# Single thresholds, leftovers loaded two tiles ahead, and a fixed order for VectorE's softmax from tile 98

## The chip, the cores and the metric

The kernel runs on one core of one Trainium2 chip. The metric is the device time of one execution in microseconds (us), the median of several runs. Beside it stands one profiled execution, in which a hardware profiler recorded the instructions of every engine: TensorE (PE, with its weight loads as PEld), VectorE (DVE), ScalarE (ACT), GpSimd (POOL) and SyncE (SP), which issues most of the loads and stores.

## What is computed

Attention with a relative threshold, and behind it a mixture of experts in which every token goes to one expert. Batch 8, 8 heads, 576 positions, head size 64; the 4608 tokens have 512 columns, and there are 8 experts with 1024 hidden columns.

```python
scores = scale * np.matmul(q, k.transpose(0, 1, 3, 2))
thresh = np.max(scores, axis=-1, keepdims=True) - tau
scores = np.where(scores >= thresh, scores, -1000000000.0)
attn = np.exp(scores - np.max(scores, axis=-1, keepdims=True))
attn = attn / (np.sum(attn, axis=-1, keepdims=True) + 1e-09)
x = (attn @ v)                       # to (4608, 512)
logits = x @ w_gate + modality_bias[modality_id]
e_idx = np.argmax(logits, axis=1)    # gate_w: softmax of logits at e_idx
for e in range(E):
    h = np.maximum(x[e_idx == e] @ w1[e], 0.0)
    out[e_idx == e] = gate_w[e_idx == e, None] * (h @ w2[e])
```

## The kernel before, in words

Attention runs in 288 **tiles**, numbered from 0, of 128 rows of scores by 576 keys. Nine tiles make a pair of heads: eight of the 512 main rows of the two heads, and one with the 64 leftover rows of both. Pair p begins at tile 9p, four pairs make a batch. A loop runs through the tiles. In tile n TensorE makes the scores (`qk_half`, line 428) in one of two PSUM buffers, `s2[n % 2]`, so that the scores of tile n+2 wait until tile n has been masked. Then follow, on VectorE the negated row **maximum** (line 461), on ScalarE the exponential (line 471), on VectorE the **threshold** (line 468, one column) and the **mask** (line 485), which multiplies the exponentials by "score >= threshold", sums the rows and is the last reader of the scores. Two tiles later TensorE transposes the masked tile (`tr`, line 513), and after each half of a pair it multiplies by v (`pv_half`, line 547).

From tile 2 to 97 the loop goes by pairs of tiles (`two` is true): the masks of an even tile and the odd one behind it are issued together. There the maxima, thresholds and masks carry an order token ("softmax"), so that VectorE keeps them in the order of the program. Up to tile 63 (`LEAD`) both thresholds of such a pair of tiles stand behind the second maximum; from 64 to 97 one small sum (line 464) makes both. From tile 98 there is no token: a planner places the instructions of VectorE, ScalarE and SP by its own estimate, while TensorE and GpSimd run in the order of the program.

**Preparing a pair** (`prep_steps`): TensorE transposes the leftovers of k and q (`kq_r`, line 351), then the main keys and queries (`k_m`, `q_m`, line 365); GpSimd splits them into high and low parts (lines 339, 340); SP copies these into place (lines 374, 380). `load_qk`, called five tiles before the preceding pair begins, issues the loads of the leftovers (line 115) and then the main ones (line 124), all on SP.

**The experts** run between the attention's instructions. After each batch the routing (`route_a`, `route_b`, `route_c`) writes the tokens' places into a table. Seven times, for a slot that begins at tile n0 (64, 100, 136, 175, 214, 253, 292), `pick` **chooses** the expert with the most waiting tokens, in eight small instructions on VectorE over eight values (lines 732 to 743), asked for at tile n0 - 14 without a token. SP reads the choice into registers; GpSimd gathers the tokens' rows (line 855) by a list that SP loads (line 839); TensorE transposes them (line 869) and multiplies by both weights (lines 915 and 942). The first layer's result leaves PSUM as a high part by ScalarE (line 926) and a low part by VectorE (line 927). The first slot has 256 tokens and two gathers, asked for 6.4 and 6.3 tiles before it begins.

**Banks**: `tbank` hands out four PSUM banks in turn, the one used longest ago first. `let_go` returns a bank that was held over several steps and puts it at the end of the line. `x_out`'s `rest` takes a bank for one small transpose (line 617), which VectorE scales (line 630).

Of the kernel before, what the change touches and what calls it, by code (L numbers as in the profile page):

```python
# [29 lines left out]
def tile_attn_moe(  # L30
# [14 lines left out]
    C = {'prep': [0, 1, 2], 'tr0': 6, 'pv0': 7, 'tr1': 12, 'sums': 13, 'pv1': 13, 'x': 14, 'gate': [15, 16, 17, 18], 'route': 18, 'routeb': 21, 'E0': 28, 'lag': 3, 'first': ((1, 0), (1, 1), (1, 2), (1, 3), (2, 0)), 'lld': {(1, 5): 15, (1, 6): 15.6, (1, 7): 16.2, (2, 5): 16.8, (2, 6): 17.4, (2, 7): 18}, 'late': ((1, 5), (1, 6), (1, 7), (2, 5), (2, 6), (2, 7)), 'pick': -14, 'vld': 6, 'qkld': -5, 'pre': 2.5, 'wl': 3.5, 'rows': -11, 'gat': [-9.5, -8.5, -7, -5], 'xt': [-6, -5, -4, -2], 'lc': 21, 't3': 84, 'neg': 1.0, 'draw': [2, 2, 2, 2, 1, 2, 2, 1, 2], 'last': 36, 'part': 84, 'join': 11, 'drawj': [2, 2, 2, 2, 2, 2, 0, 2, 2], 'gatej': [15, 15, 17, 18], 'te': 8, 'f0': 19, 'sc': 1, 'warm': 24,  # L45
         'wS': [-6, -4.7, -3.4, 3, 12.5, 14, 15.5, 21.5, 4.2, 5.4, 6.6, 7.5, 22.7, 23.8, 24.9, 25.8],
         'wL': [-5.5, -4, -2.5, 2.7, 12, 13.3, 14.6, 21, 3.8, 4.9, 6, 7.1, 15.8, 22.2, 23.4, 24.6], 'ask': 4, 'gat0': [-6.4, -6.3], 'xt0': [-2, -1], 'rows0': -9.6, 'gat1': [-9.6, -9.5, -5], 'fill': (8, 8.5), 'fpool': (3,), 'route0': (18, 18, 20), 'pair1': 5, 'rest1': 19, 'gap': (1.0, 0.75), 'exp': -12.5, 'two': 98, 'end': (12, 13, (15, 16), (13.5, 13.6, 14.1, 14.2), 14.5, 15, 16.5), 'xf': 9, 'early': [], 'parts': ((((7, 0, 2), (9, 2, 5)), ((11, 0, 2), (13, 2, 5))), (((6, 0, 2), (8, 2, 4), (10, 4, 5)), ((12, 0, 2), (14, 2, 5)))), 'xp': ((15, 16), (16, 17)), 'prepp': ((0, 1, 2), (0, 0, 2)), 'trp': ((7, 11), (6, 12))}
# [59 lines left out]
    def load_qk(p):  # L107
        b, j = p // NPAIR, p % NPAIR
        tiles = []
# [4 lines left out]
        for z, src in enumerate((k, q)):  # L114
            nc.sync.dma_start(out=r[z * R:(z + 1) * R], in_=src[b, 2 * j:2 * j + 2, SA:S, :].rearrange("s r d -> r s d"))
        for z, (nm, src) in enumerate((("k", k), ("q", q))):
# [190 lines left out]
    def tbank(hold=False):  # L307
        i = next(x for x in line if x not in held)
        line.remove(i)
        line.append(i)  # L310
        if hold:
            held.add(i)
        return banks[i]

    def let_go(t):
        for i in range(4):
            if banks[i] is t:
                held.discard(i)
                line.remove(i)
                line.append(i)  # L320
# [126 lines left out]

    def softmax_a(n, two):
# [12 lines left out]
        in_line(nc.vector.tensor_reduce(out=nm[:, 0:1], in_=sv, axis=AX.XY, op=ALU.max, negate=True), two)  # L461
# [16 lines left out]
    def softmax_b(n, two):  # L478
        p, i = n // NI, n % NI
        e, th = soft.pop(n)[1], soft.pop((n, "th"))  # L480
# [6 lines left out]
            in1=e, op0=ALU.is_ge, op1=ALU.mult, accum_out=rs[:, ia:ia + 1]), two)  # L487
# [104 lines left out]
    def x_out(p):  # L592
# [136 lines left out]
    def pick(w):  # L729

        a = tiny.tile([1, NE], F32, name="pk_a", bufs=1)
        nc.vector.scalar_tensor_tensor(out=a, in0=done, scalar=float(-U * TS), in1=base[0][0:1, :],
                                       op0=ALU.mult, op1=ALU.add)
# [559 lines left out]
```

## Time and profile before

| | before |
|---|---|
| runs, us | 1015.66, 1016.04, 1013.46 |
| median, us | 1015.66 |
| profiled execution, us | 1014.53 |
| its span from first to last instruction, us | 1012.8 |
| busy share of PE, DVE, ACT, POOL | 97%, 67%, 63%, 52% |
| mean granted TensorE clock | 0.998 |

The span is what the profile's rows cover; the execution's own time holds 1.7 us more. TensorE is nearly always busy, so the reader should look for the moments in which it is not, and for what ended each of them.

### The profile page before, as it was taken

What the parts mean: (1) busy time and instruction counts of PE and PEld (TensorE: products, weight loads), DVE (VectorE), ACT (ScalarE), POOL (GpSimd) and SP (SyncE); (2) the same over time, 40 slices, a digit from 0 to 9 for tenths busy, and PEclk for the clock granted to TensorE, in tenths of its full rate; (3) what the DMA queues carried; (4) which work ended last, traced back from release to release, by engine and by line L of the source; (5) the groups of instructions that cost most, each with busy time, mean ns of one, the idle gap of its engine ahead of it and who ended that gap; (6) DMA issues with size and microseconds to landing.
All of it is one profiled execution on the core that took longest, in us unless ns stands there. A gap on an engine that the chain in (4) does not pass through costs nothing.

```text
span 1012.8 us, 20320 instructions
## 1 busy us (share of the span) xinstructions
PE 986.9 (97%) x6556; PEld 795.0 (78%) x6556; DVE 681.9 (67%) x1696; ACT 634.7 (63%) x1448; POOL 527.6 (52%) x733
## 2 busy tenths in 40 slices
PE   7999999999998999999999999999999999999997
PEld 6777678778887887888778887788878868888885
DVE  6888977787677776777677777777676765333422
ACT  6777787776666666666667666666666635334430
POOL 4354466386537554645546554646567374534311
PEclk9999999999999999999999999999999999999999
DMA  6667587678646765575645656567665336634301
GB/s 157 154 151 171 142 186 187 171 181 203 169 127 158 195 158 148 125 201 158 181 110 143 166 157 152 140 155 198 166 154 141 95 92 181 222 103 143 105 20 44
DMA packets 207139, 152.22 MB, mean 150 GB/s; under 512 B 100110, under 2 KB 168078, under 8 KB 207024
## 3 DMA queue, kind: packets, MB, share of 16 engines
q1 hardware_dynamic: 199776, 131.74, 51.2%
q0 software_dynamic: 7248, 19.09, 6.1%
q8 instruction: 54, 0.88, 0.4%
q14 instruction: 61, 0.50, 0.2%
HBM read 80.05 MB, written 19.87 MB: 99 GB/s over the span
## 4 chain that ended last, share of the span: by engine, by line
PE 79%; issue 8%; DVE 7%; DMA 2%; POOL 2%; ACT 1%; SPq 1%; POOLq 0%; DVEq 0%; ACTq 0%
PE s L428 15%; PE bk L547 15%; PE bk L513 11%; PE bk L942 11%; PE bk L915 10%; PE pm L942 5%; PE pm L915 4%; PE bk L365 2%; DVE nm L461 2%; DVE pr L485 2%; PE bk L538 2%; PE bk L869 1%; PE bk L599 1%; PE bk L646 1%; DMA k_m<-in_k_dram 1%
## 5 line engine op out<-in xcount | busy, mean ns | idle before, releaser
L461 DVE TENSOR_REDUCE nm<-s 128x1 f32<-128x576 f32 x254 | 190.9, 752 | 101.7 <-PE s L428 94.0
L485 DVE SCALAR_TENSOR_TENSOR pr<-s,nm,e 128x576 f32<-128x576 f32 x254 | 204.8, 815 | 61.6 <-ACT e L471 56.1
L471 ACT ACTIVATE e<-s,nm 128x576 f32<-128x576 f32 x254 | 188.4, 743 | 59.8 <-DVE nm L461 49.8
L428 PE MATMUL s<-km,q 128*128 128x288 f32 x1024 | 196.5, 313 | 10.6 <-DVE pr L485 9.7
L523 ACT COPY ptm<-bk 128x512 f32<-128x512 f32 x256 | 149.3, 583 | 53.4 <-PE bk L513 49.5
L513 PE MATMUL bk<-ident,pr 128*128 128x128 f32 x1152 | 173.8, 273 | 0.0
L428 PEld LDWEIGHTS s<-km,q 128*128 128x128 f32 x1024 | 146.4, 189 | 27.7 <-DVE pr L485 22.2
L513 PEld LDWEIGHTS bk<-ident,pr 128*128 128x128 f32 x1152 | 140.6, 140 | 27.2 <-issue 6.2
L547 PE MATMUL bk<-ptm,v_m 128*64 128x320 f32 (+1 forms) x1024 | 140.7, 412 | 0.0
L901 POOL TENSOR_TENSOR w2l<-raw,w2h 128x512 fp32r<-128x512 f32 x77 | 98.3, 1286 | 32.6 <-ACT w2h L897 28.5
L547 PEld LDWEIGHTS bk<-ptm,v_m 128*64 128x64 f32 x1024 | 68.2, 136 | 50.5 <-issue 8.2
L957 POOL DMA_INDIRECT out_dram<-y,tb x37 | 37.6, 1017 | 122.2 <-DVE y L955 92.8
L502 ACT COPY rp<-pr 128x64 f32<-128x64 f32 x271 | 59.9, 248 | 41.8 <-DVE pr L485 36.6
L339 POOL CAST nk<-str 128x64 fp32r<-128x64 f32 x31 | 7.4, 238 | 144.7 <-ACT str L353 140.5
L915 PE MATMUL bk<-xh,w1h 128*128 128x512 f32 (+3 forms) x204 | 82.2, 403 | 0.1
L915 PE MATMUL bk<-xh,w1l 128*128 128x512 f32 (+3 forms) x204 | 74.1, 363 | 0.0
L915 PE MATMUL bk<-xl,w1h 128*128 128x512 f32 (+3 forms) x204 | 74.0, 363 | 0.0
L942 PE MATMUL bk<-w2h,hh 128*128 128x512 f32 x168 | 73.3, 437 | 0.0
L901 POOL TENSOR_TENSOR w1l<-raw,w1h 128x512 fp32r<-128x512 f32 x53 | 68.1, 1285 | 4.2
L942 PE MATMUL bk<-w2h,hl 128*128 128x512 f32 x168 | 66.3, 395 | 0.0
L942 PE MATMUL bk<-w2l,hh 128*128 128x512 f32 x168 | 66.1, 393 | 0.0
L901 DVE TENSOR_TENSOR w1l<-raw,w1h 128x512 fp32r<-128x512 f32 x27 | 19.3, 720 | 59.4 <-ACT w1h L897 53.3
(217 smaller groups left out, 1999.5 us busy)
## 6 DMA issues: line engine op xcount, KB each, us to landing
raw<-in_moe_w_dram SPq DMA_DIRECT2D x160, 256.0 KB
q<-nq SPq DMA_DIRECT2D x124, 256.0 KB
km<-nk SPq DMA_DIRECT2D x124, 144.0 KB
v_m<-in_v_dram SPq DMA_DIRECT2D x32, 256.0 KB
xs<-xr SPq DMA_DIRECT2D x32, 256.0 KB
k_m<-in_k_dram SPq DMA_DIRECT2D x62, 128.0 KB
q_m<-in_q_dram SPq DMA_DIRECT2D x62, 128.0 KB
vr<-in_v_dram SPq DMA_DIRECT2D x64, 16.0 KB
```

Source lines behind the costliest of these rows:

```text
L428: nc.tensor.matmul(out=sps[:, hf, 0:SH], lhsT=a, rhs=x, start=(z == 0), stop=(z == len(passes) - 1))
L461: in_line(nc.vector.tensor_reduce(out=nm[:, 0:1], in_=sv, axis=AX.XY, op=ALU.max, negate=True), two)
L471: in_line(nc.scalar.activation(out=e, in_=sv, func=AF.Exp, bias=nm[:, 0:1]), two and n < LEAD)
L485: in_line(nc.vector.scalar_tensor_tensor(out=pr.rearrange("p (a x) -> p a x", a=2), in0=s2[n % 2][:, :, 0:SH], scalar=th, in1=e, op0=ALU.i ...
L502: (nc.gpsimd.tensor_copy if 2 <= n < 46 else nc.scalar.copy)(out=state[("rp", p)][:, 2 * c + s + x, :], in_=pr[:, SA:S])
L513: nc.tensor.transpose(out=ps[:, kc * P:(kc + 1) * P], in_=pr[:, kc * P:(kc + 1) * P], identity=ident)
L523: in_line(nc.scalar.copy(out=ptm[:, s, :, (c % 2) * P:(c % 2 + 1) * P], in_=pv), n + 2 < LEAD)
L547: nc.tensor.matmul(out=o, lhsT=lhsT, rhs=rhs, start=start, stop=stop, skip_group_check=True)
L901: then(eng.tensor_tensor(out=lo, in0=raw, in1=hi.bitcast(F32), op=ALU.subtract), eng is nc.vector and (lined or late))
L915: nc.tensor.matmul(out=ps[:, 0:WT], lhsT=a[:, cs], rhs=x[:, c, :], start=(c == 0 and z == 0), stop=(c == KC - 1 and z == 2))
L942: nc.tensor.matmul(out=ps, lhsT=h[:, ts], rhs=w, start=(z == 0 and y == 0), stop=(z == F2 - 1 and y == 2))
L957: i = _inst(nc.gpsimd.indirect_dma_start(out=out, out_offset=bass.IndirectOffsetOnAxis(ap=tb[:, t, 0:1].bitcast(U32), axis=0), in_=y, in_o ...
```

## The change

Five things change.

- **Thresholds.** In tiles 2 to 63 each tile has its threshold by itself: an even tile's directly behind its maximum, an odd tile's directly ahead of its mask and so behind the even tile's mask.
- **Order.** All maxima, thresholds and masks carry the token, from tile 98 too, where they stand as maximum, threshold, mask, tile by tile.
- **The choice.** `pick` is cut into three parts, asked for at n0 - 15, n0 - 14 and n0 - 13 (before: all at n0 - 14) and placed with the late work of a tile, behind its mask; its instructions carry the token.
- **Loads.** From pair 2 on the two loads of the leftovers are asked for seven tiles before the preceding pair begins, not five (`load_rest`). The two gathers of the first slot are asked for at 8.4 and 8.3 tiles before it, not 6.4 and 6.3.
- **Banks.** From tile 98, if the bank at the end of the line was just let go, `rest` puts its own bank ahead of that one.

```diff
-'pick': -14, ... 'gat0': [-6.4, -6.3]
+'pick': (-15, -14, -13), ... 'gat0': [-8.4, -8.3]
...
+    def load_rest(p):
...
+        loads[("kq_r", p)] = r
...
+        if p == 1:
+            load_rest(p)
+        r = loads.pop(("kq_r", p))
...
-    def tbank(hold=False):
+    freed = []
+
+    def tbank(hold=False, quick=False):
         i = next(x for x in line if x not in held)
         line.remove(i)
         line.append(i)
+        if quick and line[-2] in freed:
+            line[-2:] = [i, line[-2]]
...
                 held.discard(i)
+                freed[:] = [i]
...
+    def threshold(n, nm2, two):
+        y = cols(n % 2)
+        in_line(nc.vector.tensor_scalar(out=nm2[:, 1, y], in0=nm2[:, 0, y], scalar1=-1.0, scalar2=ntau,
+                                        op0=ALU.mult, op1=ALU.add), True)
...
-        in_line(nc.vector.tensor_reduce(out=nm[:, 0:1], in_=sv, axis=AX.XY, op=ALU.max, negate=True), two)
+        in_line(nc.vector.tensor_reduce(out=nm[:, 0:1], in_=sv, axis=AX.XY, op=ALU.max, negate=True), True)
...
-        for y in () if summed or two and n % 2 == 0 else (0, 1) if two else (n % 2,):
-            in_line(nc.vector.tensor_scalar(out=nm2[:, 1, cols(y)], in0=nm2[:, 0, cols(y)], scalar1=-1.0, scalar2=ntau,
-                                            op0=ALU.mult, op1=ALU.add), two)
+        if not (summed or two and n % 2):
+            threshold(n, nm2, two)
...
+        if two and n < LEAD and n % 2:
+            threshold(n, soft[n][0], two)
...
-            in1=e, op0=ALU.is_ge, op1=ALU.mult, accum_out=rs[:, ia:ia + 1]), two)
+            in1=e, op0=ALU.is_ge, op1=ALU.mult, accum_out=rs[:, ia:ia + 1]), True)
...
-                ps = tbank()
+                ps = tbank(quick=step[0] >= C['two'])
...
-    def pick(w):
+    def pick(w, out):
...
+        def which():
...
+        def place():
...
+        def take():
...
+        return which, place, take
...
+            if p:
+                at(n0 + (-7), lambda p=p: load_rest(p + 1))
             at(n0 + C['qkld'] if p else 0, lambda p=p: load_qk(p + 1))
...
-        def choose(cells=cells, w=w):
-            cells["c"] = pick(w)
-        at(n0 + C['pick'], choose)
+        def choose(z, cells=cells, w=w):
+            if z == 0:
+                cells["f"] = pick(w, cells)
+            cells["f"][z]()
+        for z, t in enumerate(C['pick']):
+            put(n0 + t, lambda z=z, choose=choose: choose(z))
```

`which` holds the old lines 732, 734, 736 and 742, `place` 737, 739 and 741, `take` 743.

## Rows read from the trace of the kernel before

**Rows 1.** Stages: us, busy us of PE, PEld, DVE, ACT, POOL; clock; DMA.

```profile
0.00:145.00 145.00, 132.52 (x1031) 101.94 (x1031) 122.57 (x330) 109.34 (x238) 69.42 (x177) 1.00 0.68 160
145.00:238.00 93.00, 91.72 (x693) 74.37 (x694) 69.27 (x170) 65.88 (x165) 59.28 (x74) 1.00 0.74 186
238.00:810.00 572.00, 568.14 (x3931) 462.45 (x3929) 413.94 (x1046) 386.45 (x909) 316.98 (x408) 1.00 0.60 155
810.00:1012.80 202.80, 194.52 (x906) 156.23 (x904) 76.15 (x153) 73.00 (x137) 81.89 (x76) 0.99 0.37 114
```

**Rows 2.** TensorE's waits, 0 to 145 us: us in total, times, longest.

```profile
PE s L428 <- DVE pr L485: 6.8, 11, 1.5
...
PE bk L351 <- DMA kq_r<-in_q_dram: 0.8, 1, 0.8
...
PE bk L365 <- DMA k_m<-in_k_dram: 0.6, 1, 0.6
```

**Rows 3.** TensorE's waits, 145 to 238 us.

```profile
PE s L428 <- DVE pr L485: 0.7, 1, 0.7
PE bk L365 <- DMA k_m<-in_k_dram: 0.5, 1, 0.5
```

**Rows 4.** TensorE's waits, 238 to 810 us.

```profile
PE s L428 <- DVE pr L485: 2.4, 2, 2.1
PE bk L351 <- DVE hl L927: 1.1, 2, 0.6
```

**Rows 5.** VectorE's timeline, tiles 17 to 19: start us, length us, instruction, count.

```profile
45.57 0.81 DVE L485 SCALAR_TENSOR_TENSOR pr<-s,nm,e 128x576 f32<-128x576 f32 x1
...
46.69 1.58 DVE L461 TENSOR_REDUCE nm<-s 128x1 f32<-128x576 f32 x2
48.30 0.34 DVE L468 TENSOR_SCALAR nm<-nm,ntau 128x1 f32<-128x1 f32 x2
48.65 0.82 DVE L485 SCALAR_TENSOR_TENSOR pr<-s,nm,e 128x576 f32<-128x576 f32 x1
```

**Rows 6.** TensorE's timeline, scores of tiles 19 and 20; in brackets, idle before.

```profile
46.70 0.77 PE L428 MATMUL s<-km,q 128*128 128x288 f32 x4
...
49.53 0.80 PE L428 MATMUL s<-km,q 128*128 128x288 f32 x4 [0.34 <-DVE pr L485]
```

**Rows 7.** Line 468, all thresholds: ns minimum/median/maximum, first and last start.

```profile
L468 DVE TENSOR_SCALAR nm<-nm,ntau x254: 175/213/217, 9.6 to 808.3; 128x1 f32<-128x1 f32 x127
```

**Rows 8.** SP's timeline near 137 us.

```profile
136.58 2.26 SPq L115 DMA_DIRECT2D kq_r<-in_k_dram  x1
```

**Rows 9.** GpSimd's timeline, 131 to 135 us.

```profile
131.84 0.61 POOL L339 CAST nq<-st 128x512 fp32r<-128x512 f32 x1 [1.52 <-ACT st L368]
...
133.95 1.09 POOL L855 DMA_INDIRECT xg<-xs,tb  x1
```

**Rows 10.** VectorE's timeline, 304 to 308 us, tiles 121 to 123.

```profile
304.34 1.14 DVE L737 TENSOR_SCALAR pk_a<-iota,pk_r 1x8 f32<-1x8 f32 x1
...
305.86 0.74 DVE L461 TENSOR_REDUCE nm<-s 128x1 f32<-128x576 f32 x1
306.52 0.80 DVE L485 SCALAR_TENSOR_TENSOR pr<-s,nm,e 128x576 f32<-128x576 f32 x1
...
307.26 0.20 DVE L468 TENSOR_SCALAR nm<-nm,ntau 128x1 f32<-128x1 f32 x1
307.38 0.53 DVE L927 SCALAR_TENSOR_TENSOR hl<-bk,hh 128x384 fp32r<-128x384 f32 x1
```

**Rows 11.** Tile `pk_a` of the choice: ns minimum/median/maximum, first and last start.

```profile
L734 DVE SCALAR_TENSOR_TENSOR pk_a<-pk_a,iota x7: 153/153/624, 115.4 to 742.8; 1x8 f32<-1x8 f32 x7
...
L737 DVE TENSOR_SCALAR pk_a<-iota,pk_r x7: 214/289/1156, 116.4 to 743.2; 1x8 f32<-1x8 f32 x7
```

**Rows 12.** Timelines of VectorE (mask of tile 126) and TensorE (scores of tile 128).

```profile
321.89 0.82 DVE L485 SCALAR_TENSOR_TENSOR pr<-s,nm,e 128x576 f32<-128x576 f32 x1
...
323.54 0.77 PE L428 MATMUL s<-km,q 128*128 128x288 f32 x4
```

More of the change, by code (lines that the diff above doesn't have):

```diff
@@ L43, in tile_attn_moe @@
 ):
-    C = {'prep': [0, 1, 2], 'tr0': 6, 'pv0': 7, 'tr1': 12, 'sums': 13, 'pv1': 13, 'x': 14, 'gate': [15, 16, 17, 18], 'route': 18, 'routeb': 21, 'E0': 28, 'lag': 3, 'first': ((1, 0), (1, 1), (1, 2), (1, 3), (2, 0)), 'lld': {(1, 5): 15, (1, 6): 15.6, (1, 7): 16.2, (2, 5): 16.8, (2, 6): 17.4, (2, 7): 18}, 'late': ((1, 5), (1, 6), (1, 7), (2, 5), (2, 6), (2, 7)), 'pick': -14, 'vld': 6, 'qkld': -5, 'pre': 2.5, 'wl': 3.5, 'rows': -11, 'gat': [-9.5, -8.5, -7, -5], 'xt': [-6, -5, -4, -2], 'lc': 21, 't3': 84, 'neg': 1.0, 'draw': [2, 2, 2, 2, 1, 2, 2, 1, 2], 'last': 36, 'part': 84, 'join': 11, 'drawj': [2, 2, 2, 2, 2, 2, 0, 2, 2], 'gatej': [15, 15, 17, 18], 'te': 8, 'f0': 19, 'sc': 1, 'warm': 24,
+    C = {'prep': [0, 1, 2], 'tr0': 6, 'pv0': 7, 'tr1': 12, 'sums': 13, 'pv1': 13, 'x': 14, 'gate': [15, 16, 17, 18], 'route': 18, 'routeb': 21, 'E0': 28, 'lag': 3, 'first': ((1, 0), (1, 1), (1, 2), (1, 3), (2, 0)), 'lld': {(1, 5): 15, (1, 6): 15.6, (1, 7): 16.2, (2, 5): 16.8, (2, 6): 17.4, (2, 7): 18}, 'late': ((1, 5), (1, 6), (1, 7), (2, 5), (2, 6), (2, 7)), 'pick': (-15, -14, -13), 'vld': 6, 'qkld': -5, 'pre': 2.5, 'wl': 3.5, 'rows': -11, 'gat': [-9.5, -8.5, -7, -5], 'xt': [-6, -5, -4, -2], 'lc': 21, 't3': 84, 'neg': 1.0, 'draw': [2, 2, 2, 2, 1, 2, 2, 1, 2], 'last': 36, 'part': 84, 'join': 11, 'drawj': [2, 2, 2, 2, 2, 2, 0, 2, 2], 'gatej': [15, 15, 17, 18], 'te': 8, 'f0': 19, 'sc': 1, 'warm': 24,
@@ L46, in tile_attn_moe @@
          'wS': [-6, -4.7, -3.4, 3, 12.5, 14, 15.5, 21.5, 4.2, 5.4, 6.6, 7.5, 22.7, 23.8, 24.9, 25.8],
-         'wL': [-5.5, -4, -2.5, 2.7, 12, 13.3, 14.6, 21, 3.8, 4.9, 6, 7.1, 15.8, 22.2, 23.4, 24.6], 'ask': 4, 'gat0': [-6.4, -6.3], 'xt0': [-2, -1], 'rows0': -9.6, 'gat1': [-9.6, -9.5, -5], 'fill': (8, 8.5), 'fpool': (3,), 'route0': (18, 18, 20), 'pair1': 5, 'rest1': 19, 'gap': (1.0, 0.75), 'exp': -12.5, 'two': 98, 'end': (12, 13, (15, 16), (13.5, 13.6, 14.1, 14.2), 14.5, 15, 16.5), 'xf': 9, 'early': [], 'parts': ((((7, 0, 2), (9, 2, 5)), ((11, 0, 2), (13, 2, 5))), (((6, 0, 2), (8, 2, 4), (10, 4, 5)), ((12, 0, 2), (14, 2, 5)))), 'xp': ((15, 16), (16, 17)), 'prepp': ((0, 1, 2), (0, 0, 2)), 'trp': ((7, 11), (6, 12))}
+         'wL': [-5.5, -4, -2.5, 2.7, 12, 13.3, 14.6, 21, 3.8, 4.9, 6, 7.1, 15.8, 22.2, 23.4, 24.6], 'ask': 4, 'gat0': [-8.4, -8.3], 'xt0': [-2, -1], 'rows0': -9.6, 'gat1': [-9.6, -9.5, -5], 'fill': (8, 8.5), 'fpool': (3,), 'route0': (18, 18, 20), 'pair1': 5, 'rest1': 19, 'gap': (1.0, 0.75), 'exp': -12.5, 'two': 98, 'end': (12, 13, (15, 16), (13.5, 13.6, 14.1, 14.2), 14.5, 15, 16.5), 'xf': 9, 'early': [], 'parts': ((((7, 0, 2), (9, 2, 5)), ((11, 0, 2), (13, 2, 5))), (((6, 0, 2), (8, 2, 4), (10, 4, 5)), ((12, 0, 2), (14, 2, 5)))), 'xp': ((15, 16), (16, 17)), 'prepp': ((0, 1, 2), (0, 0, 2)), 'trp': ((7, 11), (6, 12))}
@@ L105, in tile_attn_moe @@
     vr2 = [glob.tile([P, 2, D], F32, name=f"vr{i}") for i in range(2)]
-    def load_qk(p):
+    def load_rest(p):
         b, j = p // NPAIR, p % NPAIR
-        tiles = []
         if p == 1:
@@ L115, in load_qk @@
             nc.sync.dma_start(out=r[z * R:(z + 1) * R], in_=src[b, 2 * j:2 * j + 2, SA:S, :].rearrange("s r d -> r s d"))
+        loads[("kq_r", p)] = r
+    def load_qk(p):
+        b, j = p // NPAIR, p % NPAIR
+        tiles = []
+        if p == 1:
+            load_rest(p)
+        r = loads.pop(("kq_r", p))
         for z, (nm, src) in enumerate((("k", k), ("q", q))):
```

20 lines of the change are left out of this document (10 added, 10 removed).

## The prediction

> **What bounds the kernel now.** I read the page's busy shares first, then a table of stages, then who waited for whom on TensorE in each stage, then the timeline around the waits that the change can reach. The stage table [rows 1] cuts the span at tile 64 (145 us), tile 98 (238 us) and the end of attention (810 us). TensorE is idle 12.5 us in the first stage (145.00 - 132.52), 1.3 us in the second, 3.9 us in the third and 8.3 us in the last: 25.9 us of 1012.8, at a granted clock of 0.99 to 1.00 throughout. So TensorE is the bound, VectorE runs at 0.85 of the first stage and 0.72 of the third, and an edit to VectorE's order is worth only the idle time of TensorE that it removes. The waits tell how much that can be. Before tile 64 the scores of a tile wait for the mask of the tile two before it, which frees their PSUM buffer: 6.8 us in 11 waits; two waits for loads cost 0.8 and 0.6 us [rows 2]. Between tiles 64 and 98 there is one wait for a mask, 0.7 us, and another for a load, 0.5 us [rows 3]. From tile 98 there are 2.4 us in two waits for a mask and 1.1 us in two waits of the leftovers' transpose for VectorE's low halves [rows 4]. That is 12.9 us within reach; the start and the 8.3 us of the tail are untouched.
>
> **Part 1, single thresholds (tiles 2 to 63).** Before, a pair runs on VectorE as maximum, maximum, threshold, threshold, mask, mask. In tiles 18 and 19 the two maxima start at 46.69, both thresholds at 48.30, the first mask at 48.65 [rows 5]. TensorE starts tile 20 at 49.53 after 0.34 us of idle time, as soon as mask 18 is through, and does so in every one of the 11 waits [rows 2, 6]. After the change the even tile's threshold stands between the maxima and the odd one between the masks. No instruction is added: there were 254 thresholds of one column, 213 ns at the median, and there are as many. From the second maximum's end (48.27) to the first mask was 0.38 us and will be about 0.03; in return the second maximum starts later by what one threshold holds VectorE. Where an independent instruction follows, that is 0.12 us (threshold 307.26, next 307.38 [rows 10]); the threshold's whole length is 0.21 [rows 7]. So the first mask comes 0.14 to 0.23 us earlier, up to 0.35 where VectorE idled between the maxima. I take 0.2. The odd mask gains this and loses it again to the threshold now ahead of it, which it must wait for (0.21): it stays where it was. What is late next is therefore the odd tile: its scores started at 46.70 [rows 6], and mask 17 had ended at about 46.38 (0.81 us from 45.57 [rows 5]), a room of 0.31, which 0.2 nearly uses up. Ten waits at 0.2 and one of 0.13 us make **2.1 us**; bounds 0 (the odd tile binds at once) and 11 x 0.35, cut by the shorter waits to 3.5.
>
> [...]
>
> **Part 2, leftovers two tiles ahead.** At tile 63 the transpose of the leftovers waits 0.8 us for their load and, once it is through, the main keys' transpose 0.5 us for theirs [rows 2, 3]. On SP the first of the two leftover loads was issued at 136.58 and held the queue 2.26 us, behind the copies of q and ahead of the main loads [rows 8]. Two tiles earlier they stand before the copies of q, for which SP has to wait for GpSimd anyway, and the main loads move up by some 2 us. Their buffer is free by then, since its one reader, a transpose, ran at the first tile of that pair. Both waits, and the 0.6 us at tile 27, a main load behind the same kind of pair [rows 2], go: 0.8 + 0.5 + 0.6 = **1.9 us**, bounds 0.3 and 1.9. The queue moved past is SP's, by two issues a pair; if it were full, what falls behind would be the copies of q, with their use some five tiles on.
>
> The first slot's two gathers move up two tiles as well. GpSimd runs in program order, so they now stand before the split of q (131.84) and not behind it (133.95) [rows 9]. Each holds GpSimd about 1.1 us; GpSimd was idle 1.52 us before that split, so the copies of q start about 1 us later, and the traffic of the gathers is then over earlier. I cost this at **0**; with that cover gone it is 1 us of stall, once.
>
> **Part 3, the order from tile 98 and the choice in three parts.** In tile 122 the eight small instructions of the choice stood between the softmax instructions: one of them took 1.14 us at 304.34, the next maximum went ahead of the mask (305.86), and the mask, started at 306.52, was 2.1 us late for TensorE [rows 4, 10]. The fixed order puts that mask ahead of the next maximum, and the choice's parts behind masks. Tile 88's wait of 0.7 us [rows 3] has the same origin one choice earlier (tiles 85 and 86), as has the 0.3 us that remains of the 2.4 [rows 4]. Of 0.7 + 2.4 = 3.1 I take **2.8 us**, bounds 1.0 and 3.1.
>
> The parts have a price. Of the eight instructions seven are like the one of 0.153 us at the median, the eighth, the one that was long, has a median of 0.29 and a maximum of 1.16 us [rows 11]: 7 x 0.15 + 0.29 = 1.3 us a choice, 2.2 with the long one. Untied, they were put where VectorE had nothing better; tied, the next maximum is queued behind each of them and the scores behind that. There are seven choices; I take two of them to fall where a mask is close to late already and to cost 0.4 us each: **-0.8 us**, bounds 0 and -3.
>
> **Part 4, the quick bank.** At tiles 108 and 126 the leftovers' transpose takes the bank that the expert matmuls have just let go, and waits for its evacuation, 1.1 us in two waits [rows 4]. The change hands it the bank of the small transpose before it instead. **1.0 us**, bounds 0 and 1.1.
>
> New waits elsewhere, since VectorE's and ScalarE's free instructions are placed anew: **-0.5 us**, bounds 0 and -2 (the third stage's whole wait for masks was 2.4).
>
> Sum: 2.1 + 1.9 + 2.8 + 1.0 - 0.8 - 0.5 = 6.5 us. The profiled execution took 1014.53 us (span 1012.8 and 1.7 around it), so 1008.0 on its scale. The median of the runs shown, 1015.66, lies 1.1 higher: **1009.1 us**.
>
> **Rivals.** (a) *The waits are replaced.* In the first stage the odd mask binds as soon as the even one is earlier (room 0.31), and in the third the planner's mistakes move to other tiles. For it: VectorE is at 0.85 there. Against it: the waits lie on even tiles alone. Only the loads' 1.9 and a little more remain: about 1013.3 us. (b) *The choice blocks VectorE at its fixed places.* If the long instruction takes 1.16 us as a rule [rows 11], each choice holds the softmax 2.2 us, and where three of the seven find no room and half of it reaches TensorE the sum loses 3.3 us more: about 1012.5. [...] (c) *Slower: strict alternation.* In 27 of the 190 tiles from 98 (the first 100, the last 284) the next maximum ran ahead of the mask, as at tile 121 [rows 10]. Tied, it comes behind. That maximum, its exponential and its mask then come at least one maximum (0.75 us) later; the smallest room behind such a tile is 0.83 us (mask 126 ends at 322.71, the scores that need its buffer start at 323.54 [rows 12]). At 0.8 us it costs nothing. From 1.6 us, where the exponential is waited for as well and ScalarE has taken up other work, eight of the 27 bind (2.8 us in all), at 2.2 us sixteen bind for 11 us: 1015.7 + 11 - 6 = about 1020 us. (d) *The order changes nothing*: in 163 of the 190 tiles it already was so. Then only the part of 3 that is the choice goes, about 1011.
>
> **How the numbers follow.** Forecast 0.55; (a) 0.20; (b) 0.08; (c) 0.10; (d) 0.07. The low end takes all upper bounds and no cost, 3.5 + 1.9 + 3.1 + 1.1 = 9.6 us, and rounds down for the 1.1 us by which the profiled execution was the faster: 1005. The high end takes in (a) and (b) and no change at all, 1015.5; (c) is left out. A measurement of this kernel tells about 0.3% (3.0 us) from no change, so faster means below 1012.6: forecast and (d), and half of (b), 0.66. Slower, above 1018.7: 0.09. Same: 0.25.
>
> **What would show it.** Right: TensorE's waits for masks before tile 64 fall from 6.8 to about 4.7 us; none for leftover loads; nothing over 0.5 us near tiles 88, 108, 123 and 126; TensorE's idle time in the span about 19 us. Wrong: as many waits before tile 64, now on odd tiles (a); waits of 0.5 to 1 us just behind the choice's instructions (b); some ten or more short waits for masks between 238 and 810 us (c); GpSimd idle before the gathers near 131 us while the split of q stands behind them.

## The result, and the profile after

The changed kernel takes **1021.53 us** in the median of five runs (1020.21 to 1023.16); the kernel before, on the same chip, 1015.66 us (1012.95 to 1016.49). The ratio is 1.0067, 95% interval 1.0051 to 1.0082: slower by 0.7%, where the prediction said 1009.1 us and at most 1015.5. The profiled execution of the changed kernel took 1020.21 us, its span is 1018.5 us.

In the changed kernel the scores have line 440, the maximum 478, the exponential 487, the threshold 462, the mask 503, the low half 952. First the stages, which answer [rows 1] (us, busy us of PE, PEld, DVE, ACT, POOL; clock; DMA):

```profile
0.00:145.00 145.00, 136.99 (x1052) 104.67 (x1053) 125.81 (x332) 111.11 (x242) 71.40 (x182) 1.00 0.68 164
145.00:238.00 93.00, 92.59 (x699) 75.00 (x697) 70.87 (x174) 66.41 (x166) 57.23 (x69) 1.00 0.72 186
238.00:815.00 577.00, 567.85 (x3905) 458.56 (x3905) 416.25 (x1044) 389.86 (x906) 317.80 (x408) 1.00 0.60 153
815.00:1018.50 203.50, 194.67 (x907) 156.37 (x905) 75.65 (x149) 72.64 (x135) 81.30 (x75) 0.99 0.37 113
```

TensorE idles 8.0 us before 145 us (12.5 in [rows 1]) and 0.4 us up to 238 (1.3): in idle time, what was expected there came. From 238 us to the end of attention, now 815, it idles 9.2 us, where it had idled 3.9. Its waits in the first and in the third stage, against [rows 2, 4] (us in total, times, longest), say for what:

```profile
PE s L440 <- DVE pr L503: 3.9, 5, 1.1
...
PE s L440 <- DVE nm L478: 0.5, 1, 0.5
```

```profile
PE s L440 <- DVE pr L503: 7.0, 13, 0.8
PE bk L556 <- DVE hl L952: 1.1, 1, 1.1
PE bk L531 <- DVE xr L648: 0.5, 1, 0.5
```

From tile 98 two waits for a mask (2.4 us, 2.1 of it in one) have become thirteen (7.0 us), none over 0.83. These are the "ten or more short waits for masks" that the prediction named as the sign of rival (c).

Idle time is not all that such a wait costs. From the scores of tile 99 to those of tile 287 the changed kernel takes 7.8 us longer than the kernel before, but is idle only 4.8 us more (8.6 against 3.9); for the other 3 us TensorE counts as busy (565.2 against 562.1 us for the same 3891 matmuls, at a granted clock of 1.00). In dense work the record of a matmul runs on into the next one by up to some 0.25 us (in the kernel before four transposes from 50.16 to 50.76, the next scores from 50.52), and that much of a wait doesn't show: the step from tile 113 to 114 grew by 0.93 us, with 0.69 us of idle time.

How one of them comes about is read from VectorE's timeline at tiles 102 and 103 (start us, length us, instruction, count; in brackets, idle before and what ended it):

```profile
247.12 0.82 DVE L503 SCALAR_TENSOR_TENSOR pr<-s,nm,e 128x576 f32<-128x576 f32 x1 [0.29 <-ACT e L487]
...
247.87 0.75 DVE L478 TENSOR_REDUCE nm<-s 128x1 f32<-128x576 f32 x1
248.66 0.21 DVE L462 TENSOR_SCALAR nm<-nm,ntau 128x1 f32<-128x1 f32 x1
249.49 0.82 DVE L503 SCALAR_TENSOR_TENSOR pr<-s,nm,e 128x576 f32<-128x576 f32 x1 [0.62 <-ACT e L487]
```

and from ScalarE's and TensorE's beside it, the exponential of tile 103, then the scores of tiles 104 and 105:

```profile
248.71 0.74 ACT L487 ACTIVATE e<-s,nm 128x576 f32<-128x576 f32 x1 [0.29 <-DVE nm L478]
```

```profile
248.01 0.80 PE L440 MATMUL s<-km,q 128*128 128x288 f32 x4
...
250.37 0.80 PE L440 MATMUL s<-km,q 128*128 128x288 f32 x4 [0.61 <-DVE pr L503]
```

The mask of tile 102 starts at 247.12, the maximum of 103 right behind it (247.87), ScalarE takes the exponential as soon as the maximum is there (248.71, ends at 249.45), and only then can mask 103 start (249.49). So from mask to mask 2.37 us pass, with nothing in them that could be left out: 0.75 for the mask's turn, 0.75 for the maximum, 0.74 for the exponential and some 0.13 for the hand-overs. The scores of tile 105 start 0.06 us after mask 103 is through (250.31): TensorE runs at the pace of this chain. The scores of tile 103 had been ready at 246.43, 1.44 us before VectorE came to their maximum. In the kernel before VectorE did this in the same block:

```profile
243.88 0.76 DVE L461 TENSOR_REDUCE nm<-s 128x1 f32<-128x576 f32 x1
...
244.85 0.76 DVE L461 TENSOR_REDUCE nm<-s 128x1 f32<-128x576 f32 x1
245.62 0.82 DVE L485 SCALAR_TENSOR_TENSOR pr<-s,nm,e 128x576 f32<-128x576 f32 x1
...
246.67 0.82 DVE L485 SCALAR_TENSOR_TENSOR pr<-s,nm,e 128x576 f32<-128x576 f32 x1
```

The maximum of tile 101 (244.85) goes ahead of mask 100 (245.62), its exponential runs beside that mask, and mask 101 follows 1.05 us after mask 100, not 2.37. One exchange, and the lateness is gone: mask 101 is through 1.38 us before the scores of tile 103 start (in the changed kernel, 0.06).

### The profile page after: what moved, and what is told of

Same layout as the page of the kernel before. It is cut to its first block, busy times and chain, and to the rows that moved or that the text cites. A ratio compares the mean times of both kernels' runs of the same rounds, so it can differ in the third digit from the quotient of the medians.

```text
span 1018.5 us, 20317 instructions
## 1 busy us (share of the span) xinstructions
PE 992.1 (97%) x6556; PEld 794.6 (78%) x6556; DVE 688.6 (68%) x1696; ACT 640.0 (63%) x1448; POOL 527.7 (52%) x733
## 4 chain that ended last, share of the span: by engine, by line
PE 74%; DVE 10%; issue 8%; ACT 5%; POOL 2%; DMA 1%; POOLq 0%; ACTq 0%; DVEq 0%
PE bk L565 15%; PE s L440 14%; PE bk L531 10%; PE bk L967 9%; PE bk L940 8%; PE pm L967 5%; PE pm L940 4%; DVE pr L503 4%; ACT e L487 3%; DVE nm L478 2%; PE bk L377 2%; PE bk L556 1%; PE bk L894 1%; PE bk L617 1%; PE bk L664 1%
## 5 line engine op out<-in xcount | busy, mean ns | idle before, releaser
L503 DVE SCALAR_TENSOR_TENSOR pr<-s,nm,e 128x576 f32<-128x576 f32 x254 | 207.3, 816 | 96.5 <-ACT e L487 93.3
L880 POOL DMA_INDIRECT xg<-xs,tb x37 | 39.2, 1058 | 52.1 <-DMA tb<-tab 20.9
```

The lines of the kernel that those rows point to most:

```text
L503: in_line(nc.vector.scalar_tensor_tensor(out=pr.rearrange("p (a x) -> p a x", a=2), in0=s2[n % 2][:, :, 0:SH], scalar=th, in1=e, op0=ALU.i ...
L880: nc.gpsimd.indirect_dma_start(out=xg, out_offset=None, in_=xs[0:nrow, :], in_offset=bass.IndirectOffsetOnAxis(ap=box["tb"][:, t, 0:1].bit ...
```

## The experiments

Each line of the table below compares the start of a tile's scores with that in the thresholds-alone kernel (second run of it), in us later (+) or earlier; it is worked out from TensorE's timeline in each trace. "End" is the span. The trace of the kernel before holds 1.7 us of a stall at tile 54, told of below, that the other columns don't have.

| tile | thresholds alone, us | before | changed | order at one choice | order at seven | early parts | work in shade | work on path |
|---|---|---|---|---|---|---|---|---|
| 54 | 120.2 | +3.0 | +0.5 | +0.5 | +0.3 | +0.2 | +1.5 | +0.4 |
| 72 | 161.6 | +3.7 | +1.1 | +0.5 | +0.3 | +3.2 | +3.7 | +1.9 |
| 99 | 236.1 | +3.5 | +0.1 | -0.6 | -0.7 | +3.1 | +2.7 | +0.9 |
| 126 | 315.0 | +3.5 | +0.5 | -2.7 | -2.9 | +4.8 | +4.1 | +5.8 |
| 162 | 423.9 | +3.5 | +1.1 | -2.9 | -3.1 | +4.7 | +4.8 | +10.7 |
| 207 | 560.9 | +3.5 | +3.4 | -2.7 | -1.0 | +4.7 | +7.3 | +17.9 |
| 287 | 801.8 | +3.9 | +8.3 | -2.7 | -0.2 | +4.7 | +11.2 | +26.8 |
| end | 1009.7 | +3.1 | +8.8 | -2.3 | +0.3 | +4.5 | +11.4 | +27.9 |

### Which part costs

Three theories stood at the start, all read from the trace of the changed kernel. A: the fixed order costs, by the chain just shown, and what is left of the change gains. B: what costs is that the choice's three parts are tied. C: the quick bank brings the transposes into new waits.

The changed kernel **without the order from tile 98**:

```diff
-        in_line(nc.vector.tensor_reduce(out=nm[:, 0:1], ...), True)
+        in_line(nc.vector.tensor_reduce(out=nm[:, 0:1], ...), two)      # threshold and mask alike
```

> The changed kernel with one part undone: from tile 98 maxima, thresholds and masks carry no order token, as before; the choice stays in three parts, the loads, thresholds and the quick bank stay. Theory A (strict alternation: from tile 98 each maximum stands behind the mask of the tile before it, and maximum, exponential and mask then form one chain of 0.75 + 0.8 + 0.82 = 2.4 us a tile that has no slack for VectorE's other work): the 7.8 us that the changed kernel lost between tiles 99 and 287 come back in most part, about 1013 to 1015 us, and TensorE's waits for masks from tile 98 fall from 7.0 us in 13 to under 3. Theory B (the choice's parts, tied in place, hold the softmax): stays at 1020 or above, since the parts keep their place. Theory C (the quick bank makes the next user wait): stays within 1 us of 1021.

1019.43 us, ratio 1.0018 (1.0004 to 1.0032). The loss goes down from 0.67% to 0.18%; from tile 99 to 287 this trace loses 1.2 us against that of the kernel before, the changed kernel 7.8. It is short of theory A's time because TensorE waited 4.2 us at tile 52 and 1.2 us for the copies of q at tile 63, and lost 1.6 us at a lower granted clock behind tile 123 (a mean of 0.96 from 290 to 330 us, 1.00 in the kernel before); all three are taken up below.

**The order alone**, in the kernel before (the reverse edit there):

> The kernel before with one part of the change alone: maxima, thresholds and masks carry the token from tile 98. Theory A: 6 to 8 us slower than before, about 1022 to 1024 us, with the loss spread over tiles 99 to 287 and nothing changed before tile 98. Theories B and C: within 2 us of before, 1014 to 1017.

1022.4 us, ratio 1.0051 (1.0032 to 1.0071), and eleven waits for masks from tile 98, 5.8 us. The order by itself is slower than not having it, its gain at tile 123 included.

The changed kernel with **the choice as it was** (one piece, no token):

> The changed kernel with the choice as before: eight instructions in one piece, without the token. Theory A: within 2 us of the changed kernel, 1020 to 1023 us. Theory B: 4 us or more faster than the changed kernel, about 1016 or below.

1023.3 us, ratio 1.0062 (1.0038 to 1.0087): no better. The tied choice is not the main cause. It has a share: from tile 99 to 287 this trace loses 6.6 us against that of the kernel before, as the order alone does (6.4), and the changed kernel 7.8.

The changed kernel **without the quick bank**:

```diff
-                ps = tbank(quick=step[0] >= C['two'])
+                ps = tbank()
```

> The changed kernel without the quick bank. In its trace the bank that was put back made the next users wait 1.05 us at tile 120 and some 0.2 to 0.5 us at tiles 168, 258 and 287, against the 1.1 us that it was to save. Theory C: 2 us or more faster than the changed kernel, 1019 or below. Theories A and B: within 1 us of it, since 1.1 us of waits for VectorE's low halves at tiles 108 and 126 return.

1026.95 us, ratio 1.0095 (1.007 to 1.0119). The bank is not the cause either. With the order it is worth nothing: from tile 99 to 287 this trace loses 7.9 us against that of the kernel before, the changed kernel 7.8. What it is slower by lies in a wait of 4.3 us at tile 52, of the same kind, and in a stretch at a granted clock of 0.50 that begins in it and lasts from 120 to 126 us.

### Is it the chain?

A theory that blames a chain can be put to the test by giving VectorE the same useless work at two places. **In the shade**: one more instruction a tile from tile 98, between maximum and mask, where VectorE waits for the exponential. **On the path**: the same between mask and next maximum.

```diff
+    def idle_work():
+        in_line(nc.vector.tensor_reduce(out=extra_t, in_=ident, axis=AX.X, op=ALU.max), True)
...
         if not (summed or two and n % 2):
             threshold(n, nm2, two)
+        if n >= C['two']:          # in the shade; on the path: behind the mask in softmax_b
+            idle_work()
```

> The changed kernel with one more VectorE instruction a tile from tile 98, 190 in all: a maximum over 128 columns of a constant, about 0.2 us, in the fixed order between a tile's maximum and its mask, where VectorE waits 0.87 us (median) for the exponential. It does nothing that is needed. Theory A (serial chain mask, maximum, exponential, mask): it lies beside the exponential and costs 0 to 2 us. Rival (VectorE's total work binds): 190 x 0.2 us = 38 us of work cost as much here as between mask and maximum.

> The same unneeded instruction of about 0.2 us a tile, but between a tile's mask and the next maximum. Theory A (serial chain): it lengthens the chain by 0.2 us in each of the 105 tiles in which the next maximum follows its mask at once; carried along from tile to tile with the measured rooms behind the masks that makes 11 us (counted tile by tile, without carrying it along, the 30 tiles with a room under 0.1 us would give 5). So some 1032 us, at least 8 us above the run with the instruction beside the exponential. Rival (VectorE's total work binds): the same time as that run.

In the shade 1022.36 us, ratio 1.0072 (1.0057 to 1.0086), as without it; on the path 1041.35 us, ratio 1.0266 (1.025 to 1.0283). The instruction's row on the path (ns minimum/median/maximum; in the shade the median is 276), and TensorE's waits for masks from 238 us, first in the shade, then on the path:

```profile
L109 DVE TENSOR_REDUCE extra<-ident x190: 273/280/283, 238.1 to 833.0; 128x1 f32<-128x128 f32 x190
```

```profile
PE s L444 <- DVE pr L509: 6.7, 13, 0.8
```

```profile
PE s L444 <- DVE pr L507: 14.8, 26, 1.1
```

The same 53 us of VectorE's time (190 x 0.28) cost 0.5 us, which is within the noise, at one place and 20 us (0.0199 x 1015) at the other. So VectorE's total work does not bind; the serial chain does, and that is shown, not argued. The size came out above my 11 us: I had carried the delay along with the rooms of the unlengthened chain, and more tiles joined it as it grew (26 waits, not 13). Counted tile by tile it would have been 5.

Does any fixed order do? **Maximum n+1 always ahead of mask n**, tied as much:

```diff
+            if C['two'] < n <= NSTEP:
+                softmax_b(n - 1, two)     # right behind softmax_a(n)
```

> The changed kernel, but from tile 98 the token's order is maximum of tile n+1, then mask of tile n (the changed kernel: mask n, then maximum n+1). Everything is as much tied as in the changed kernel. Theory A (a chain mask, maximum, exponential, mask of about 2.37 us a tile, in which VectorE waits for ScalarE, is what the alternation costs): the exponential leaves the chain, the loss from tile 99 to tile 287 falls from 7.8 us to 2 or less, and the time to about 1014 to 1016 us. Rival B (what costs is that VectorE's instructions are tied at all, so that other work finds no place): no better than the changed kernel, 1020 us or more. Rival C (the mask now stands behind a maximum that waits for the next tile's scores, so it frees its buffer later): slower than the changed kernel, above 1025 us, with more than 15 waits of the scores for masks from tile 98 on.

1063.27 us, ratio 1.0479 (1.046 to 1.0498); rival C, and theory A's number was wrong (TensorE's waits from 238 us):

```profile
PE s L440 <- DVE pr L503: 30.8, 62, 1.4
```

Now each mask waits behind a maximum that waits for the next tile's scores, and those scores are in the chain themselves. Neither order is good in every tile; the planner's 27 exceptions among 190 were of use because they came where the scores were early: in 26 of the 27 the next tile's scores were through before the tile's exponential was, elsewhere in 16 of 162.

### The early parts

**Thresholds alone**, and a second time on another chip:

```diff
-        for y in () if summed or two and n % 2 == 0 else (0, 1) if two else (n % 2,):
-            in_line(nc.vector.tensor_scalar(out=nm2[:, 1, cols(y)], ...), two)
+        if not (summed or two and n % 2):
+            threshold(n, nm2, two)
...
+        if two and n < LEAD and n % 2:
+            threshold(n, soft[n][0], two)
```

> The kernel before with the single thresholds alone. Theory A (the prediction's part 1): 2.1 us less, about 1015 us beside 1017.2 for the kernel before, TensorE's waits for masks before tile 64 at 4 to 5 us (6.8 before), and a gain that grows evenly from tile 9 to tile 63. Rival (odd masks bind as soon as even ones are earlier): no gain, waits for masks still 6 to 7 us, now on odd tiles. Rival (the stall at tiles 52 to 54 comes with the thresholds' place): 2 us slower, about 1019 us.

> The thresholds alone once more, unchanged, beside the kernel with the order around one choice. As at the first time: ratio 0.996 to 0.998. If TensorE's increments come late at 115 to 120 us in this execution too, TensorE waits 1 to 4 us more at tiles 52 to 54 and the ratio is 0.997 to 0.999.

1011.96 us, ratio 0.9968 (0.9956 to 0.998), and 1013.2 us, ratio 0.9981 (0.997 to 0.9991): 1.9 to 3.2 us gained, a version that beats both kernels. Its waits before tile 64 are those of the changed kernel (3.9 us in 5), and the waits for leftover loads at tile 63 are gone without any load having been moved.

**Thresholds, leftovers and gathers early** (no order, old choice, old bank), then **the gathers back** at their place, then **with the quick bank**:

> The change without the fixed order from tile 98, without the choice's three parts and without the quick bank: what is left is the single thresholds, the leftovers two tiles earlier and the first gathers two tiles earlier. Theory A (these parts gained 3.4 us by tile 98 in the changed kernel's trace, and the order from tile 98 took it back): 3.4 us below the kernel before, some 1013.5 us, with the scores of tile 99 about 3 us earlier than in the kernel before. Rival (the 4.2 us wait of TensorE at tile 54, which the run without the order showed, belongs to one of these parts): about 1017 us, with TensorE idle 2 to 4 us more at tiles 52 to 54 than before.

> Single thresholds and early leftovers, with the first slot's gathers back at 6.4 and 6.3 tiles (the run with the gathers two tiles earlier gave a ratio of 0.9999, thresholds alone 0.9968). Theory G (the gathers, put ahead of the split of q on GpSimd, made the copies of q late at tile 63, by 2.0 us there): the wait for the copies of q at tile 63 is gone, the split of q stands ahead of the gathers again, and the ratio is 0.996 to 0.997. Rival L (the two leftover loads, now on SP ahead of the copies of q, make them late): a wait of 2 us for the copies of q stays, ratio 0.999 to 1.000.

> The change without the fixed order from tile 98 and without the choice's three parts: single thresholds, early leftovers and gathers, and the quick bank. Theory A: 3.4 us from the early parts and 1.0 us from the bank, about 1012.5 us; against the kernel without the bank 1 us less. Rival (the bank is worth the 2.8 us by which the changed kernel without it was slower): about 1011 us. Rival (a stall of 4 us at tiles 52 to 54 comes with the early parts): about 1016 us.

1015.04 us, ratio 0.9999 (0.9988 to 1.001); 1013.75 us, 0.9992 (0.9982 to 1.0002); 1015.32 us, 1.0007 (0.9995 to 1.0019). What the thresholds had won is gone, in the first and third with a wait of 2.0 and 2.9 us for the copies of q at tile 63, in the second with one of 1.1 us: theory G and rival L each hold a part. Why the third waits 0.9 us more than the first stays open. SP's timeline in the early-parts kernel, and TensorE's at tile 63:

```profile
125.08 0.95 SPq L897 DMA_DIRECT2D raw<-in_moe_w_dram  x2
126.14 0.68 SPq L114 DMA_DIRECT2D kq_r<-in_k_dram  x1
126.91 2.56 SPq L392 DMA_DIRECT2D km<-nk  x4
129.51 0.65 SPq L114 DMA_DIRECT2D kq_r<-in_q_dram  x1
130.37 0.48 SPq L897 DMA_DIRECT2D raw<-in_moe_w_dram  x1
132.24 3.92 SPq L386 DMA_DIRECT2D q<-nq  x4
```

```profile
139.86 0.77 PE L440 MATMUL s<-km,q 128*128 128x288 f32 x4 [1.99 <-DMA q<-nq]
```

and with thresholds alone SP's timeline, then GpSimd's split of q and first gather:

```profile
124.47 1.52 SPq L885 DMA_DIRECT2D raw<-in_moe_w_dram  x3
126.15 3.11 SPq L380 DMA_DIRECT2D km<-nk  x4
129.64 3.50 SPq L374 DMA_DIRECT2D q<-nq  x4
```

```profile
128.33 1.29 POOL L340 TENSOR_TENSOR nq<-st,nq 128x512 fp32r<-128x512 f32 x1
129.77 1.09 POOL L861 DMA_INDIRECT xg<-xs,tb  x1 [0.15 <-DMA raw<-in_moe_w_dram]
```

With the loads early, one weight load of 256 KB has moved from ahead of the copies of k to directly ahead of the copies of q, and with the gathers early GpSimd splits q 2.6 us later (130.94 against 128.33). The copies are asked for at 132.24, not 129.64, and the scores of tile 63 need them at 137.9. With the quick bank the waits for low halves at tiles 108 and 126 are not in the trace, but the 1.1 us are not won: beside thresholds alone these two steps are 0.7 us shorter each, the next ones 0.46 us longer each, since the scores of tiles 110 and 128 now wait for a mask, and the step to tile 172 is 0.24 us longer. That leaves 0.2 us.

How much of this sits in the changed kernel? **The changed kernel with loads and gathers as before**:

> The changed kernel with the leftover loads and the first gathers where the kernel before has them. Theory A (the loss is the order's; in the changed kernel's own trace the copies of q were late by 0.5 us at most): 0 to 1 us better than the changed kernel, ratio 1.006 to 1.007. Rival (the early loads and gathers cost in the changed kernel the 3 us that they cost with the thresholds alone): ratio 1.0035 to 1.0045.

1024.68 us, ratio 1.0075 (1.0054 to 1.0095): no better than the changed kernel, but its trace holds a wait of 2.4 us at tile 52, of the same kind as above. At tile 63 it is 0.7 us quicker, which is what the early loads and gathers cost in the changed kernel. There SP asked for the copies of q as late (132.51) as in the early-parts kernel, but tile 63 waited only 0.46 us. Why it waits less there I can't say.

### The order only where it helps

**Order at all seven choices**, in six tiles each (thresholds, quick bank and three parts kept, loads and gathers as before), then **at one choice** (tiles 120 to 125, the later choices untied), then the latter once more beside thresholds alone:

```diff
+    def near(n):
+        return any(b - 16 <= n <= b - 11 for b in begins)      # one choice: b = begins[2] = 136
...
-        in_line(..., True)
+        in_line(..., two or near(n))
```

> Single thresholds, the quick bank and the choice in three parts, but the fixed order only in the six tiles around each choice (n0 - 16 to n0 - 11); loads and gathers as in the kernel before. Theory A (the order is worth its gain at the choices, 2.1 us at tile 123, and costs along the chain everywhere else): the 2.1 us wait at tile 123 is gone, the chain costs under 1 us, ratio about 0.992 to 0.995, below the thresholds alone. Rival (the chain costs as much at the choices as it gains): 0.997, as the thresholds alone. Rival (the choice's tied parts cost): 0.999 or more.

> Single thresholds, the quick bank, and the fixed order only in the six tiles around the choice that made TensorE wait 2.1 us (tiles 120 to 125); the choices behind it in three parts but without the token. Loads and gathers as in the kernel before. The run with the order at all seven choices stood 2.6 us ahead of thresholds alone at tile 162 and gave it back by the end. Theory A (the order pays only where a mask was late, and costs along the chain everywhere else): all waits from tile 128 to 287 stay as in the run with thresholds alone, the 2.1 us at tile 123 and the two 0.56 us for the low halves are gone, ratio 0.994 (about 1009 us). Rival (a choice in three parts costs by itself, without order): 0.997 or more.

> The kernel with the order around one choice once more, unchanged, on the same chip as the thresholds alone. By the traces the two should differ by 2.1 us (tile 123), 0.8 to 1.0 (tile 88) and 1.1 us (low halves at tiles 108 and 126): if the first run's wait of 3.7 us at tile 52 is not there, 3 to 4 us below the thresholds alone, ratio 0.993 to 0.994; if it is there again, no better than they.

At seven: 1012.76 us, ratio 0.998 (0.997 to 0.9989). At one: 1014.1 us, 0.9966 (0.9952 to 0.9979), and the second time **1009.63 us, 0.9946 (0.9933 to 0.9959)**, 3.6 us below thresholds alone on the same chip and the fastest version found. TensorE's waits from 238 us in that kernel, and with thresholds alone:

```profile
PE s L439 <- DVE pr L505: 0.9, 4, 0.3
PE bk L533 <- DVE xr L650: 0.5, 1, 0.5
```

```profile
PE s L428 <- DVE pr L491: 2.4, 2, 2.1
PE bk L351 <- DVE hl L933: 1.1, 2, 0.6
```

The traces show where: 0.98 us at tile 88, 1.94 at tile 123. At the four choices behind tile 162 the kernel tied at seven gives back 2.9 us (-3.1 to -0.2 at tile 287), in waits at tiles 163, 204, 280 and 281. These four are in every trace in which the order and the choice in three parts are tied there, and in none with the order and the choice in one piece: what costs there is the tied choice. In the changed kernel VectorE's timeline ahead of mask 161, and TensorE's at tile 163:

```profile
423.86 0.87 DVE L756 SCALAR_TENSOR_TENSOR pk_a<-done,pos 1x8 f32<-1x8 f32 x1
...
425.21 0.74 DVE L478 TENSOR_REDUCE nm<-s 128x1 f32<-128x576 f32 x1
...
426.81 0.82 DVE L503 SCALAR_TENSOR_TENSOR pr<-s,nm,e 128x576 f32<-128x576 f32 x1 [0.55 <-ACT e L487]
```

```profile
427.69 0.80 PE L440 MATMUL s<-km,q 128*128 128x288 f32 x4 [0.67 <-DVE pr L503]
```

Four instructions of the choice hold the maximum back by 1.35 us (423.86 to 425.21), and the mask of the tile comes too late for the scores of tile 163.

Between tiles 99 and 287 the kernel with the order everywhere falls 10.4 us behind the one with six tied tiles (+0.1 to +8.3 against -0.6 to -2.7). That is the price of the order and of the tied choice together. The order alone, in the kernel before, loses 6.4 us there, with the 2.0 us that it wins at tile 123 already in it: 8.4 us. The tied choice in three parts adds some 1.3 us, by the traces with the old choice and with the new.

### A stall that does not belong to the kernel

**The kernel before once more**, for a second trace:

> The kernel before, unchanged, for another trace of it. In the trace that the prediction read, TensorE waited 1.8 us at tiles 53 and 54, and the semaphore increments of its matmuls at 115 to 120 us were recorded up to 1.3 us after the matmuls had ended; in the traces of the thresholds alone and of the changed kernel neither is seen. If that stall belongs to the kernel before, it is there again; if it belongs to the execution, TensorE waits under 0.7 us at tiles 53 and 54 and the gain of the thresholds by tile 72 against this trace is 1.8 us smaller, about 1.5 us.

The wait at tile 54 is there again (1.88 us), which by the expectation would speak for the kernel. But the kernel with the order at one choice has two traces too, of the same instructions; TensorE's waits from 100 to 145 us, first and second time:

```profile
PE bk L533 <- ACT ptm L543: 3.7, 1, 3.7
PE s L439 <- DVE pr L505: 1.1, 2, 0.9
```

```profile
PE s L439 <- DVE pr L505: 1.2, 2, 0.9
PE bk L376 <- ACT xh L340: 0.4, 1, 0.4
```

So the stall comes and goes with the same instructions. These two traces are from two chips, and the stall goes with the group of kernels that were measured together, not with the kernel. In the traces that hold it (both of the kernel before; those without the order, of the order alone, with the old choice, without the bank and with the old loads; the first of the order at one choice) the semaphore increments of TensorE's matmuls at 115 to 120 us were recorded up to 4.4 us after the matmuls' ends, and some 5% of all increments are missing from the trace; in the others they come 0.01 us after. Seven of these eight are all the traces of two groups, and no trace of the other three groups has it. The medians of the kernel before in the five groups say the same: 1017.17 and 1017.65 us in the two with the stall, 1015.11 to 1015.26 in the three without. It costs the kernels of a group unequally (waits of 1.8 to 4.3 us), so the ratios of those without the order, without the bank and with the order at one choice (first time) hold a part of it. What sets it off stays open. That is why I compare tiles before 72 only between traces of one kind.

## Why the prediction was wrong, step by step

**Part 1 had the idle time right, and in part by luck.** Without the wait at tile 54, which comes and goes with the stall (1.1 of the 6.8 us in [rows 2], 0.3 of the 3.9 after), the waits for masks fell from 5.7 to 3.6 us: 2.1, as said. But they did not fall by 0.2 us each: six went whole (0.25 to 0.37 us), the two of 1.46 us lost 0.31 each, and the one at tile 48 grew by 0.43. (One of the eleven was on an odd tile, tile 3.) And rival (a) held in part. The odd masks do bind now, as here mask 19 for the scores of tile 21, which start 0.05 us behind its end (49.79) without any idle time that shows:

```profile
48.97 0.82 DVE L503 SCALAR_TENSOR_TENSOR pr<-s,nm,e 128x576 f32<-128x576 f32 x1 [0.15 <-ACT e L487]
```

```profile
49.84 0.80 PE L440 MATMUL s<-km,q 128*128 128x288 f32 x4
```

In the kernel before the scores of 14 tiles up to 63 start within 0.08 us of the end of the mask they need, one of them odd; in the changed kernel 22, twelve of them odd. So on the timeline the masks win about 1 us up to tile 72, and the two waits for loads, which went with the thresholds alone, 1.3; together that fits the 1.9 to 3.2 us by the clock.

**Part 2 was wrong twice.** The waits for loads in [rows 2, 3] went with the thresholds alone, so there was nothing left to win. And "if it were full, what falls behind would be the copies of q, with their use some five tiles on" had the use wrong: asked for some 130 us, needed at 137.9. The gathers' "1 us of stall, once" was right in mechanism and size: with them back the wait at tile 63 falls from 2.0 to 1.1 us, and that rest comes with the loads. In the changed kernel itself both together cost 0.5 to 0.7 us.

**Part 3 was right in its gain and near in its price.** The gain is 2.9 us at tiles 88 and 123, against 2.8. The traces tell it apart: the wait at tile 88, where the order always was, is gone wherever the choice is in three parts; the one at tile 123 is 2.0 to 2.1 us wherever the order is missing there, three parts or not. The price of the choice's parts, 0.8, is 1.3 us by the traces; the medians (old choice: 1.0062, new: 1.0067) can't tell. So rival (b) held in small: the long instruction is now another of the choice's, 0.87 us at tile 161, and the wait of 0.67 us at tile 163 stands behind it. What made that instruction long, no run shows.

**Part 4 took idle time for time.** The two waits went, 1.1 us, but what followed them waited in their place, and 0.2 us were won without the order. With the order the two waits go as well, bank or no bank, and another of 1.1 us for the same low halves comes at tile 120. Net nothing there.

**The step that failed is the cost of the order.** The sum put it at nothing, by rival (c)'s "At 0.8 us it costs nothing"; the nearest term, new waits elsewhere, was -0.5 us with bounds 0 and -2. I had asked of each of the 27 tiles by itself whether a mask 0.8 us later meets a room of 0.83 or more, and every tile passed. Both halves of that were wrong. The mask is later than that: mask 101 follows mask 100 after 2.58 us (242.18 to 244.76), not 1.05, so by 1.5 us, since its maximum now comes behind mask 100 and its exponential behind that. And the delay isn't spent at each tile: a late mask makes the next maximum late, that the next exponential, and that the next mask, at 2.37 us a tile. TensorE of the kernel before asked for tiles 103 to 105 after 2.37, 2.10 and 1.59 us, so the chain does not catch up there; it does where a block of matmuls with v gives 4 to 6 us of room. The measured price of the order alone is 8.4 us (6.4 with its gain at tile 123), not 0.5. Rival (c) had place, sign and time (about 1020 us) right and got 0.10, because I priced it by a delay from which the exponential is waited for "as well", while in the chain it nearly always is: from tile 98, 172 of 190 masks start within 0.06 us of the end of their exponential, before 129. VectorE's idle time ahead of the mask says the same in one row (busy us, mean ns; idle before, and what ended it), before and after:

```profile
L485 DVE SCALAR_TENSOR_TENSOR pr<-s,nm,e 128x576 f32<-128x576 f32 x254 | 204.8, 815 | 61.6 <-ACT e L471 56.1 <-issue 1.6 <-DVE nm L468 1.2
```

```profile
L503 DVE SCALAR_TENSOR_TENSOR pr<-s,nm,e 128x576 f32<-128x576 f32 x254 | 207.3, 816 | 96.5 <-ACT e L487 93.3
```

The sum as measured, trace against trace: 3.4 us gained up to tile 99 (1.3 of it because the trace before holds the stall at tile 54 and this one does not), 7.8 lost from there to tile 287 (6.4 to the order, 1.3 to the tied choice), and 1.3 lost behind it, of which 0.5 is a wait for `xr` and the rest stays open. That makes 5.7 us, the difference of the spans; the medians differ by 5.9.

## What to carry to other kernels

Before you tie an order that the planner broke in some places, follow the chain that the order makes (here mask, maximum, exponential, mask) through a whole dense block and compare its length a tile with the pace of the bounding engine; rooms looked at one by one hide a delay that is handed on. Tie only where a trace shows something late: six tiles gave 1.9 us at tile 123, 190 tiles lost 6.4 with that gain in it. Don't read a gain or a loss from idle time alone: look at when the next tile starts. And before you move a load ahead, look at what falls behind it on the same queue, and when that is used.

## What the hardware showed beside this

In one execution two waits of TensorE cost more than their length. In the early-parts kernel the 2.0 us wait at tile 63 and the 2.1 us wait at tile 123, which every kernel without order there has, were both followed by a stretch at about half of the granted clock, 0.50 from 141 us and 0.54 to 0.61 from 308 us, where it had been 1.00 (stages of 1 us, then of 2; columns as in the stages above, the clock third from the end):

```profile
139.00:140.00 1.00, 0.14 (x1) 0.17 (x2) 0.00 (x0) 0.13 (x1) 0.26 (x1) 1.00 1.26 196
140.00:141.00 1.00, 1.00 (x9) 1.00 (x10) 0.33 (x1) 0.00 (x0) 0.00 (x0) 0.96 1.30 220
141.00:142.00 1.00, 1.00 (x7) 0.67 (x7) 1.00 (x2) 0.48 (x1) 0.00 (x0) 0.50 0.71 128
```

```profile
306.00:308.00 2.00, 1.10 (x8) 0.94 (x10) 2.00 (x6) 1.42 (x4) 1.70 (x3) 1.00 1.00 220
308.00:310.00 2.00, 2.00 (x10) 0.98 (x10) 1.34 (x5) 1.20 (x3) 1.75 (x3) 0.54 0.78 215
310.00:312.00 2.00, 2.00 (x10) 0.86 (x8) 0.53 (x2) 0.00 (x0) 1.91 (x3) 0.61 0.03 7
```

Of the eight traces with the 2.0 to 2.1 us wait at tile 123, three have such a stretch behind it (the mean granted clock of these executions is 0.994 to 0.995, of the other five 0.998 to 0.999). In the second trace of thresholds alone the clock stayed at 1.00:

```profile
303.00:305.00 2.00, 1.16 (x8) 0.97 (x10) 2.00 (x6) 1.48 (x4) 1.69 (x3) 1.00 0.97 217
305.00:307.00 2.00, 2.00 (x18) 1.02 (x16) 1.34 (x5) 1.14 (x3) 1.76 (x2) 1.00 0.84 214
```

The table shows what it cost: from tile 99 to 126 the early parts fall 1.6 us behind thresholds alone (+3.1 to +4.8) with the same wait in both. So one wait of 2 us costs 2 in one execution and 3.7 in another.
